# Key features times values: two heads a product, four chunks a burst, and the sums of keys made by transfers

## The chip, the cores and the metric

The kernel runs on one core of one Trainium2 chip. The metric is the device time of one execution in microseconds; the kernel before took 514.9 us, the median of three runs (514.82 to 515.21). The chip's engines run side by side, each through its own instructions in order: TensorE (PE) does matrix products, VectorE (DVE) and ScalarE (ACT) work element by element, GpSimd (POOL) does a little elementwise work and can issue transfers, and SyncE (SP) issues most of the transfers. SBUF is the on-chip memory with 128 partitions, PSUM the memory that TensorE writes into.

## The reference

Two branches share the input x (2048 rows of 512) and are mixed by a gate per row.

```python
pq, pk = per-head linear of q and k          # 32 heads of 16
phi_q = concat(softmax(pq), softmax(-pq))    # 32 features a head
phi_k = concat(softmax(pk), softmax(-pk))
kv  = einsum("bhsf,bhsd->bhfd", phi_k, v)    # a 32 x 16 matrix a head, summed over the 2048 rows
z   = einsum("bhsf->bhf", phi_k)             # the sum of the key features over the rows
num = einsum("bhqf,bhfd->bhqd", phi_q, kv)
den = einsum("bhqf,bhf->bhq", phi_q, z)[..., None] + 1e-6
a   = (num / den) @ wo
b   = relu(x @ w1 + b1) ** 2 @ w2 + b2       # 512 -> 1792 -> 512
out = g * a + (1 - g) * b,  g = sigmoid((x * gate_w).sum(-1))
```

The change is about `kv` and `z`, and about how the folded weights of the queries get back from a helper's layout.

## The kernel before

Rows come in 16 chunks of 128, four to a block, and the 1792 hidden units in 14 tiles. The program makes two sweeps over the four blocks, each with seven of the hidden tiles: 56 steps. A step is the up product of one hidden tile for 512 rows (`u`, 12 matmuls of 128x512), two steps ahead, and the down products of the present one (`d`, 12 matmuls). Every large product is three matmuls of split operands (high times high, high times low, low times high), all in one helper (lines 70 to 72).

The attention work is put between these steps by a table of slots (`at(slot, ...)`, two slots to a step); Tile's scheduler then orders each engine's instructions. In the first sweep each chunk has a projection `k` (with the key's per-head linear already folded into the weight), a softmax pair on DVE and ACT that leaves `phi` (128 rows x 1024 features) in a tile `e`, and a projection `v`, which ACT copies into `vext`: per head 16 values and a seventeenth column of ones. After every second chunk, `do_kv` runs a burst: per chunk and head one small matmul with 17 columns of `vext` as weights and 32 columns of `phi` streaming through, 32 of them a chunk, on the four 32-column strips of the PE array in turn. All chunks add into one PSUM bank `kvps`. The column of ones makes `z` in the same products: it is each head's seventeenth row.

After the last burst `kv_done` copies `kvps` out on DVE, sends the rows of `z` through DRAM so that they come back broadcast to all partitions (`zbc`, for the denominators on POOL in the second sweep), transposes the rest on PE (`kvt`) and writes it into `kvb`, the weights for the queries' numerators (`num`, line 400: 16 matmuls of 256 columns for each pair of chunks, on eight tiles of the array).

Besides, DVE folds the queries' per-head linear into their weight during the first sweep: 64 steps (`foldq_step`), each with a broadcast load `wqr` and a multiply-add into `row`; after every 16 steps DVE transposes the accumulated row (line 241) into a tile `wqt`, and at slot 46 four SP transfers with 512-byte pieces (line 245) write it into DRAM as `wqm`, from where four loads (line 249) bring the folded weights back. They are split into high and low parts (`wqh` on ACT, `wql` on DVE) for the first `q` projection right after the first sweep.

SP's transfers are issued in order: one that waits holds all behind it. So are the instructions of ACT and DVE.

Of the kernel before, what the change touches and what calls it, by code (L numbers as in the profile page):

```python
# [8 lines left out]
F32 = mybir.dt.float32  # L9
F32R = mybir.dt.float32r  # L10
AF = mybir.ActivationFunctionType
ALU = mybir.AluOpType
# [11 lines left out]
NFH = NF // 2  # L24
LAG = 2
NG = 8
VW = DH + 1
NV = 3
AHEAD = 150


# [1 line left out]
def tile_gated_mix(ctx: ExitStack, tc: tile.TileContext, xT, xn, wqT, wkT, wphi, wv, wo, w1, b1, w2, b2, gw, out):  # L33
# [110 lines left out]
    hold = pool("hold", NV)  # L144
# [15 lines left out]
    vext = [hold.tile([P, H * VW], F32, tag="vz", name=f"vext{i}") for i in range(NV)]  # L160
    heads = lambda v: v.rearrange("p (h v) -> p h v", v=VW)
    for v in vext:
        nc.gpsimd.memset(heads(v)[:, :, DH:VW], 1.0)
    zbc = []


# [59 lines left out]
    def foldq_step(i):  # L226
        g, e = divmod(i, DH)
        t = stage.tile([P, 512], F32, tag="in", name="wqr")
        nc.sync.dma_start(t, wqT.rearrange("(j e) g d -> g e j d", e=DH)[g, e].unsqueeze(1).to_broadcast([8, DH, D]))
        s = st["phc"][:, g, e:e + 1]  # L230
        with tc.issue_after(st["low"].ins):
            if e == 0:
                st["acc"] = row()
                nc.vector.tensor_scalar(st["acc"], t, s, None, ALU.mult)
            else:
                nc.vector.scalar_tensor_tensor(st["acc"], t, s, st["acc"], op0=ALU.mult, op1=ALU.add)  # L236
        if e == DH - 1:
            if g == 0:
                st["wqt"] = work.tile([P, 2, 4, NG, 32], F32, tag="phiT", name="wqt", bufs=1).rearrange(
                    "p u r g s -> p (u r g s)").rearrange("p (c g j) -> p c g j", c=4 * NK, g=NK)  # L240
            nc.vector.transpose(st["wqt"][:, :, g, :], st["acc"].rearrange("p (c j) -> p c j", c=4 * NK))

    def foldq_move():
        for r in range(4):
            nc.sync.dma_start(wqm.rearrange("c i (r n) -> r i c n", r=4)[r],
                              st["wqt"][32 * r:32 * r + 32].rearrange("p c g j -> p c (g j)"))
        st["wq"] = [row() for _ in range(NK)]
        for k in range(NK):
            nc.sync.dma_start(st["wq"][k], wqm[4 * k:4 * k + 4].rearrange("c i n -> (c i) n"))
# [43 lines left out]


    def gate_load(n):
        t = st["xn", n] = work.tile([P, D], F32, tag="ol" if n % 2 else "oh", name="xn", bufs=2)
        nc.sync.dma_start(t, xn[n])

    def gate_dot(n):
# [20 lines left out]
            mm3(ps, xs[k], ws[k], sc, ALL, k == 0, k == NK - 1)  # L320
        return ps

    def exps(ps, tag="e"):
# [4 lines left out]
        e = work.tile([P, H, 2, DH], F32, tag=tag, name="e", bufs=2 if tag == "e" else 1)  # L328
        bc = lambda t: t.unsqueeze(2).to_broadcast([P, H, DH])
        with tc.high_priority(offset=AHEAD):  # L330
            nc.vector.tensor_reduce(mx, pv, AX.X, ALU.max)
            nc.vector.tensor_reduce(mn, pv, AX.X, ALU.min)
            nc.vector.tensor_tensor(e[:, :, 0, :], pv, bc(mx), ALU.subtract)
            nc.vector.tensor_tensor(e[:, :, 1, :], bc(mn), pv, ALU.subtract)  # L334
# [13 lines left out]


    def kv_chunk(n, kvps, phi, v):  # L350
        for i in range(NG):
            for j in range(4):
                h = 8 * (i % 4) + 4 * (i // 4) + j
                nc.tensor.matmul(kvps[32 * j:32 * j + VW, 32 * i:32 * i + 32], v[:, h * VW:(h + 1) * VW],
                                 phi[:, 32 * h:32 * h + 32],
                                 start=(n == 0 and i == 0), stop=(n == NB * NC - 1),
                                 skip_group_check=True)

    def q_phi(n, e3, r):
        ez = work.tile([P, 2 * H, DH], F32, tag="ez", name="ez", bufs=1)  # L360
# [161 lines left out]
    def do_k(b, c):  # L522

        n = b * NC + c
        e3, r = exps(project(c, st["x", b], st["wa"], "k"), "ez" if n % NV == NV - 1 else "e")
        st["phi", n] = scaled(e3, r, nc.vector)

    def do_v(b, n, c):
        ps = project(c, st["x", b], st["wb"], "v")
        with tc.high_priority(offset=AHEAD):  # L530
            nc.scalar.activation(heads(vext[n % NV])[:, :, :DH], ps.rearrange("p (h f) -> p h f", f=DH), AF.Copy)

    def do_kv(n):
        if n == 0:
            st["kv"] = ps_b.tile([P, 2 * P], F32, tag="s", name="kvps")
        for m in (n, n + 1):
            kv_chunk(m, st["kv"], st["phi", m], vext[m % NV])

    def do_q(b, n, c):
        st["q", n] = exps(project(c, st["x", b], st["wa"], "q"))  # L540
# [8 lines left out]
        st["o", pair] = numer(st["pt", pair])  # L549

    def kv_done():
        kvps, kvs = st["kv"], row()[:, :2 * P]
        nc.gpsimd.memset(kvs, 0.0)
        for j in range(4):
            s = slice(32 * j, 32 * j + VW)
            with tc.high_priority(offset=AHEAD):
                nc.vector.tensor_copy(kvs[s, :], kvps[s, :])
        zr = zrow.rearrange("(i q j f) -> q j i f", i=4, q=2, f=32)
        for q in range(2):
            nc.sync.dma_start(zr[q], kvs[DH::32, q * P:(q + 1) * P].rearrange("p (i f) -> p i f", f=32))  # L560
        for half in range(2):
            z = hold.tile([P, H * VW], F32, tag="vz", name=f"z{half}")[:, :D]
# [7 lines left out]
        for j in range(4):  # L570
            s = slice(32 * j, 32 * j + 32)
            with tc.high_priority(offset=AHEAD):
                nc.vector.tensor_copy(kvb[s, :, DH * (j % 2):DH * (j % 2 + 1)], kt[s, :, :DH])

    def finish(n, c):
        ps = attended(st["o", n // 2], n % 2, st["wb"])
# [31 lines left out]
        at(5 + k // 2, v_ready, k)  # L608
    for b in range(NB):
        for c in range(NC):  # L610
            s = b * SL + 3 * c - 5 if b else 3
            at(s, gate_load, b * NC + c)
            at(s + 3 if b else 7 + c, gate_dot, b * NC + c)
            at(s + 5 if b else 9 + c, gate_chunk, b * NC + c)
        at(b * SL + 6, x_save, b)
        if b < NB - 1:
            at(b * SL + 4, x_fetch, b + 1)
# [2 lines left out]
        for c in range(NC):  # L620
# [13 lines left out]
    at(base + 11, do_w, wo, "o")  # L634
# [132 lines left out]
```

## Time and profile before

| What | Value |
|---|---|
| median of 3 runs | 514.9 us |
| the profiled execution's own time | 515.47 us |
| its span, first to last instruction | 513.7 us |
| PE busy | 509.4 us, 99% |
| DVE / ACT / POOL busy | 401.0 / 227.3 / 44.1 us |
| granted TensorE clock | 1.000 |
| moved by transfers | 75.35 MB, 147 GB/s |

The page shows one execution. A busy PE is not necessarily a PE at its peak, since the ends of its matmuls are modelled: what it really costs is read from the distances between starts. A row of the groups gives line, engine, operation, output and inputs, shapes and count, then the busy time and the mean length of one, then the idle time of the engine ahead of it and what ended that. A row of the timeline gives the start, the length and the count of instructions merged into it.

### The profile page before, as it was taken

The numbers are of one execution on the slowest core, as the hardware profiler recorded it, in microseconds if no ns is written. First come the engines' busy times: TensorE is split into PE (matmuls) and PEld (weight loads), VectorE is DVE, ScalarE is ACT, GpSimd is POOL, SyncE is SP. The second block draws the span as 40 slices with busy tenths as digits, with TensorE's granted clock in tenths as the row PEclk, the third lists the DMA queues.
The fourth block names the chain that finished last, engine by engine and source line by source line (L and its number), as shares of the span: only waits on it lengthen the run. The fifth ranks groups of instructions, "written<-read, shape, count | busy, mean of one in ns | idle before, by whom it ended". The sixth has DMA issues, their size and how long they took to land.

```text
span 513.7 us, 9257 instructions
## 1 busy us (share of the span) xinstructions
PE 509.4 (99%) x3536; PEld 411.3 (80%) x3536; DVE 401.0 (78%) x680; ACT 227.3 (44%) x390; POOL 44.1 (9%) x44
## 2 busy tenths in 40 slices
PE   9999999999999999999999999999999999999997
PEld 4888888888888888888888878788787878788876
DVE  3779769796998798787889787988779677797724
ACT  6676253254224344253854544242625353343530
POOL 1000000000000000000003040301111111201100
PEclk9999999999999999999999999999999999999999
DMA  8897535467554476548359152213153321032102
GB/s 300 290 329 236 160 119 161 142 210 245 201 157 147 156 255 223 189 139 225 107 167 342 40 163 77 92 42 103 35 167 106 85 77 48 3 101 82 41 24 82
DMA packets 48277, 75.35 MB, mean 147 GB/s; under 512 B 7016, under 2 KB 15464, under 8 KB 48232
## 3 DMA queue, kind: packets, MB, share of 16 engines
q1 hardware_dynamic: 47912, 74.35, 45.7%
q8 instruction: 28, 0.46, 0.4%
q10 hardware_dynamic: 288, 0.39, 0.2%
q14 instruction: 17, 0.14, 0.1%
q0 software_dynamic: 32, 0.01, 0.0%
HBM read 50.60 MB, written 17.83 MB: 133 GB/s over the span
## 4 chain that ended last, share of the span: by engine, by line
PE 98%; ACT 1%; DVE 0%; issue 0%
PE d L70 10%; PE u L70 10%; PE d L72 10%; PE d L71 10%; PE u L71 10%; PE u L72 10%; PE v L70 3%; PE k L70 3%; PE k L72 3%; PE q L70 3%; PE att L70 3%; PE q L71 3%; PE k L71 3%; PE att L72 3%; PE att L71 3%; PE q L72 3%
## 5 line engine op out<-in xcount | busy, mean ns | idle before, releaser
L435 ACT ACTIVATE r<-u,b1c 128x512 f32<-128x512 f32 x56 | 38.6, 689 | 163.0 <-PE u L72 162.6
L70 PE MATMUL d<-w2h,hh 128*128 128x512 f32 x222 | 86.7, 391 | 0.0
L72 PE MATMUL d<-w2h,hl 128*128 128x512 f32 x222 | 86.5, 389 | 0.0
L71 PE MATMUL d<-w2l,hh 128*128 128x512 f32 x222 | 86.4, 389 | 0.0
L70 PE MATMUL u<-xh,w1h 128*128 128x512 f32 x216 | 84.8, 393 | 0.0
L71 PE MATMUL u<-xl,w1h 128*128 128x512 f32 x216 | 84.1, 389 | 0.0
L72 PE MATMUL u<-xh,w1l 128*128 128x512 f32 x216 | 84.0, 389 | 0.0
L65 DVE TENSOR_TENSOR hl<-r,hh 128x512 fp32r<-128x512 f32 x56 | 37.8, 675 | 34.5 <-ACT hh L62 34.5
L339 DVE TENSOR_REDUCE sm<-e 128x64 f32<-128x1024 f32 x32 | 38.9, 1215 | 27.8 <-ACT e L336 27.8
L363 POOL TENSOR_TENSOR ez<-e,z 128x512 f32<-128x512 f32 x32 | 41.9, 1330 | 216.9 <-ACT e L336 210.8
L236 DVE SCALAR_TENSOR_TENSOR row<-wqr,phc,row 128x512 f32<-128x512 f32 x60 | 44.5, 742 | 6.6 <-DMA wqr<-in_wqT 6.2
L70 PEld LDWEIGHTS u<-xh,w1h 128*128 128x128 f32 x216 | 40.5, 188 | 11.1 <-issue 2.1
L70 PEld LDWEIGHTS d<-w2h,hh 128*128 128x128 f32 x222 | 41.7, 188 | 9.2 <-issue 0.6
L72 PEld LDWEIGHTS d<-w2h,hl 128*128 128x128 f32 x222 | 41.7, 188 | 8.7
L71 PEld LDWEIGHTS d<-w2l,hh 128*128 128x128 f32 x222 | 41.7, 188 | 8.6
L72 PEld LDWEIGHTS u<-xh,w1l 128*128 128x128 f32 x216 | 40.6, 188 | 8.5
L71 PEld LDWEIGHTS u<-xl,w1h 128*128 128x128 f32 x216 | 40.5, 188 | 8.2
L336 ACT ACTIVATE e<-e 128x1024 f32<-128x1024 f32 x32 | 33.8, 1057 | 24.0 <-DVE e L334 23.8
L387 ACT ACTIVATE phiT<-tb 32x256 f32<-32x256 f32 x64 | 26.5, 414 | 32.5 <-DVE tb L381 31.8
L62 ACT ACTIVATE hh<-r 128x512 fp32r<-128x512 f32 x56 | 35.3, 630 | 1.5
L436 ACT ACTIVATE r<-r 128x512 f32<-128x512 f32 x56 | 35.2, 628 | 1.1
L365 DVE TENSOR_REDUCE dz<-ez 128x64 f32<-128x1024 f32 x16 | 19.3, 1207 | 9.5 <-POOL ez L363 9.4
(116 smaller groups left out, 875.1 us busy)
## 6 DMA issues: line engine op xcount, KB each, us to landing
wqr<-in_wqT SPq DMA_DIRECT2D x64, 256.0 KB
in<-in_w SPq DMA_DIRECT2D x24, 256.0 KB
phiT<-tb SPq DMA_DIRECT2D x192, 32.0 KB
xin<-in_xT SPq DMA_DIRECT2D x16, 256.0 KB
xn<-in_xn SPq DMA_DIRECT2D x16, 256.0 KB
xkept<-xh SPq DMA_DIRECT2D x16, 256.0 KB
xkept<-xl SPq DMA_DIRECT2D x16, 256.0 KB
part<-row SPq DMA_DIRECT2D x16, 256.0 KB
```

The source lines that it names most:

```text
L62: i = nc.scalar.activation(hi, src, AF.Copy)
L65: st["low"] = elo.tensor_tensor(lo, src, hi.bitcast(F32), ALU.subtract)
L70: nc.tensor.matmul(o, ah[:, sa], bh[:, sb], start=first, stop=False)
L71: nc.tensor.matmul(o, ah[:, sa], bl[:, sb], start=False, stop=False)
L72: return nc.tensor.matmul(o, al[:, sa], bh[:, sb], start=False, stop=last)
L236: nc.vector.scalar_tensor_tensor(st["acc"], t, s, st["acc"], op0=ALU.mult, op1=ALU.add)
L336: nc.scalar.activation(ef, ef, AF.Exp)
L339: nc.vector.tensor_reduce(sm, e3, AX.X, ALU.add)
L363: nc.gpsimd.tensor_tensor(ez[:, hs, :], e3[:, hs, :], zbc[half], ALU.mult)
L387: nc.scalar.activation(dst, src, AF.Copy)
L435: nc.scalar.activation(r, ps, AF.Relu, bias=b1c[:, fc:fc + 1])
L436: nc.scalar.activation(r, r, AF.Square)
```

## The change

- **Products.** A small matmul now takes the values of two heads (32 columns, no column of ones) as weights and streams the features of the same two heads (64 columns in two pieces of 32). Half of the result, one head's values with the other head's features, is not used. A chunk has 16 of these instead of 32. `vext` becomes `val` (512 columns, with ACT's copy putting the head pairs side by side).
- **Bursts.** One burst after every fourth chunk instead of every second. For this five chunks' `phi` and `val` are kept instead of three: two more `e` tiles in the tile that the numerators use later (`ebig`), two more `val` tiles in the tag `ol`, which the gate's loads used (they now have two buffers instead of four, and other slots in the first block).
- **Sums of keys.** For chunks 0 to 14 a GpSimd transfer writes `phi` into the DRAM tile `zacc`, from chunk 1 on with an accumulating transfer (128 x 8 pieces of 512 bytes). At chunk 15 SP loads `zacc` into `zsum`, and behind the last burst `z_sum` multiplies `zsum` and the last `phi` by ones: eight matmuls with 256 columns into the other half of the PSUM bank.
- **Query fold.** Each quarter is transposed into a row of its own and stored right away by four GpSimd transfers with 128-byte pieces (16 in all). The four loads of `wqm` stay on SP.
- **After the bursts.** One DVE copy of the whole PSUM bank instead of four of 17 partitions, no `memset`, one transfer of `z` instead of two.

```diff
-VW = DH + 1
-NV = 3
+NV = 5
+    zacc = dram.tile([P, 2 * D], F32, name="zacc")
+    val = [hold.tile([P, D], F32, tag="vz", name=f"val{i}") for i in range(3)]
+    val += [work.tile([P, D], F32, tag="ol", name=f"val{i}", bufs=2) for i in range(3, NV)]
@@ foldq_step
-            nc.vector.transpose(st["wqt"][:, :, g, :], st["acc"].rearrange("p (c j) -> p c j", c=4 * NK))
-    def foldq_move():
-        for r in range(4):
-            nc.sync.dma_start(wqm.rearrange("c i (r n) -> r i c n", r=4)[r],
-                              st["wqt"][32 * r:32 * r + 32].rearrange("p c g j -> p c (g j)"))
+            t = row()
+            nc.vector.transpose(t, st["acc"])
+            for r in range(4):
+                nc.gpsimd.dma_start(wqm.rearrange("c i (r g j) -> r g i c j", r=4, g=NK)[r, g],
+                                  t[32 * r:32 * r + 32].rearrange("p (c j) -> p c j", j=32))
+    def foldq_load():
@@ kv_chunk
-        for i in range(NG):
+        ph = phi.rearrange("p (a g f) -> p a g f", a=4, f=2 * DH)
+        for i in range(4):
             for j in range(4):
-                h = 8 * (i % 4) + 4 * (i // 4) + j
-                nc.tensor.matmul(kvps[32 * j:32 * j + VW, 32 * i:32 * i + 32], v[:, h * VW:(h + 1) * VW],
-                                 phi[:, 32 * h:32 * h + 32],
+                m, g = i % 2, 4 * (i // 2) + j
+                nc.tensor.matmul(kvps[32 * j:32 * j + 32, 64 * i:64 * i + 64],
+                                 v[:, 64 * g + 32 * m:64 * g + 32 * m + 32], ph[:, 2 * m:2 * m + 2, g, :],
+    def z_keep(n):
+        nc.gpsimd.dma_start(zacc, st["phi", n], max_dma_last_dim=512, **({"accum_op": ALU.add} if n else {}))
+    def z_sum(kvps, parts):
+        one = nc.const_aps.tensor(1.0, (P, 32), F32)
+        for i, t in enumerate(parts):
+            for j in range(4):
+                nc.tensor.matmul(kvps[32 * j:32 * j + 32, 256:512], one, t[:, 256 * j:256 * j + 256],
+                                 start=i == 0, stop=i == len(parts) - 1, skip_group_check=True)
@@ do_k
+        if n < NB * NC - 1:
+            z_keep(n)
+        else:
+            st["z"] = work.tile([P, 2 * D], F32, tag="tb", name="zsum", bufs=2)
+            nc.sync.dma_start(st["z"], zacc)
@@ do_kv
-        for m in (n, n + 1):
-            kv_chunk(m, st["kv"], st["phi", m], vext[m % NV])
+        for m in range(n, n + 4):
+            kv_chunk(m, st["kv"], st["phi", m], val[m % NV])
+        if n == NB * NC - 4:
+            z_sum(st["kv"], (st["z"], st["phi", n + 3]))
@@ the table of slots
-            if c % 2:
-                at(s + 5, do_kv, n - 1)
+            if c == NC - 1:
+                at(s + 4.5, do_kv, n - 3)
-    at(46, foldq_move)
+    at(46, foldq_load)
```

**The last burst, on PE.** `kvps` is the PSUM bank of the small products, `u` and `d` the up and down products, `kvt` the transposes of `kv_done`. Before:

```order
L72 MATMUL u<-xh_3_2649,w1l_2532 128x512
L354 MATMUL kvps<-e,vext_113 17x32 x32
L354 MATMUL kvps<-e,vext_111 17x32 x32
L70 MATMUL d_2493<-w2h_645,hh 128x512
L71 MATMUL d_2493<-w2l_646,hh 128x512
```

and now, at the same place:

```order
L71 MATMUL u<-xh_3_2482,w1l_2364 128x512
L355 MATMUL kvps<-e,val_114 32x64 x16
L355 MATMUL kvps<-ebig,val_115 32x64 x16
L355 MATMUL kvps<-ebig,val_116 32x64 x16
L355 MATMUL kvps<-e,val_112 32x64 x16
L370 MATMUL kvps<-zsum,const-float32-1.0 32x256 x4
L370 MATMUL kvps<-e,const-float32-1.0 32x256 x4
L69 MATMUL d_2325<-w2h_645,hh 128x512
L70 MATMUL d_2325<-w2l_646,hh 128x512
L71 MATMUL d_2325<-w2h_645,hl 128x512
L69 MATMUL d_2326<-w2h_645,hh 128x512
L595 MATMUL kvt<-ident,row 128x128 x2
```

A burst has 64 small matmuls as before, now for four chunks, and the last one has eight of 256 columns behind it; `kvt` stands four matmuls behind the burst, where eight stood before.

**The end of the first sweep, on DVE.** `sm` and the scaled `e` belong to the last chunk's `phi`, `wql` is the split of the folded query weights, `wol` that of the output weights, `hl` the hidden units' low part. Before:

```order
L339 TENSOR_REDUCE sm<-e 128x64
L65 TENSOR_TENSOR hl<-r,hh 128x512
L341 RECIPROCAL r<-sm 128x64
L303 SCALAR_TENSOR_TENSOR xn,lg<-xn,gwb 128x512
L345 TENSOR_TENSOR e<-e,r 128x1024
L65 TENSOR_TENSOR w1l_2870<-in,w1h_2869 128x512
L65 TENSOR_TENSOR w2l_2876<-in,w2h_2875 128x512
L65 TENSOR_TENSOR wql_2864<-row,wqh_2863 128x512
```

and now:

```order
L339 TENSOR_REDUCE sm<-e 128x64
L64 TENSOR_TENSOR hl<-r,hh 128x512
L64 TENSOR_TENSOR wql_2635<-row,wqh_2634 128x512
L64 TENSOR_TENSOR wql_2677<-row,wqh_2676 128x512
L341 RECIPROCAL r<-sm 128x64
L64 TENSOR_TENSOR wql_2693<-row,wqh_2692 128x512
L345 TENSOR_TENSOR e<-e,r 128x1024
L299 SCALAR_TENSOR_TENSOR xn,lg<-xn,gwb 128x512
L64 TENSOR_TENSOR wql_2801<-row,wqh_2800 128x512
```

Three of the four splits of the query weights now stand ahead of the last `phi`, not behind it.

**The end of GpSimd's transfers and SP's issue behind them, in the changed kernel** (POOL; before, it had no transfer here):

```order
L364 DMA zacc<-e 128x8x128
L364 DMA zacc<-ebig 128x8x128
L239 DMA wqm<-row 32x16x32 x2
L364 DMA zacc<-ebig 128x8x128
L239 DMA wqm<-row 32x16x32 x2
```

The last transfer of `phi` (chunk 14) stands between the halves of the fold's last quarter. On SP the load of `zsum`, two loads of `wo` and then the four loads of `wqm` stand behind it, and then the other loads of `wo`. DVE's copy of `kv_done` stands behind the split of the third tile of `wo`.

More of the change, by code (lines that the diff above doesn't have):

```diff
@@ L295, in gate_load @@
     def gate_load(n):
-        t = st["xn", n] = work.tile([P, D], F32, tag="ol" if n % 2 else "oh", name="xn", bufs=2)
+        t = st["xn", n] = work.tile([P, D], F32, tag="oh", name="xn", bufs=2)
         nc.sync.dma_start(t, xn[n])
@@ L321, in project, with e_tile, exps @@
         return ps
-    def exps(ps, tag="e"):
+    def e_tile(tag, bufs):
+        return work.tile([P, H, 2, DH], F32, tag=tag, name="e", bufs=bufs)
+    def exps(ps, e=None):
         pv = ps.rearrange("p (h f) -> p h f", f=DH)
@@ L327, in exps @@
         mn = small.tile([P, H], F32, tag="mn", name="mn")
-        e = work.tile([P, H, 2, DH], F32, tag=tag, name="e", bufs=2 if tag == "e" else 1)
+        if e is None:
+            e = e_tile("e", 2)
         bc = lambda t: t.unsqueeze(2).to_broadcast([P, H, DH])
@@ L524, in do_k @@
         n = b * NC + c
-        e3, r = exps(project(c, st["x", b], st["wa"], "k"), "ez" if n % NV == NV - 1 else "e")
-        st["phi", n] = scaled(e3, r, nc.vector)
+        i = n % NV
+        if n == 3:
+            big = work.tile([P, 2, 4, NG, 32], F32, tag="phiT", name="ebig", bufs=1)
+            st["ebig"] = big.rearrange("p u r g s -> p (u r g s)")
+        if i < 2:
+            e = e_tile("e", 2)
+        elif i == 2:
+            e = e_tile("ez", 1)
+        else:
+            e = st["ebig"][:, (i - 3) * 2 * D:(i - 2) * 2 * D].rearrange("p (h t f) -> p h t f", t=2, f=DH)
+        e3, r = exps(project(c, st["x", b], st["wa"], "k"), e)
+        st["phi", n] = scaled(e3, r, nc.vector)
+        if n < NB * NC - 1:
+            z_keep(n)
+        else:
+            st["z"] = work.tile([P, 2 * D], F32, tag="tb", name="zsum", bufs=2)
+            nc.sync.dma_start(st["z"], zacc)
     def do_v(b, n, c):
@@ L551, in kv_done @@
     def kv_done():
[L552 to L560, printed above, removed]
+        kvs = row()
+        with tc.high_priority(offset=AHEAD):
+            nc.vector.tensor_copy(kvs, st["kv"])
+        nc.sync.dma_start(zrow.rearrange("(j f) -> j f", j=4), kvs[::32, 256:512])
         for half in range(2):
-            z = hold.tile([P, H * VW], F32, tag="vz", name=f"z{half}")[:, :D]
+            z = hold.tile([P, D], F32, tag="vz", name=f"z{half}")
             nc.sync.dma_start(z, zrow[half * D:(half + 1) * D].partition_broadcast(P))
```

23 lines of the change are left out of this document (9 added, 14 removed).

## The prediction

> **What bounds the kernel now.** I read the page first: busy shares, slices and the chain.
>
> ```profile
> span 513.7 us, 9257 instructions
> PE 509.4 (99%) x3536; PEld 411.3 (80%) x3536; DVE 401.0 (78%) x680; ACT 227.3 (44%) x390; POOL 44.1 (9%) x44
> POOL 1000000000000000000003040301111111201100
> DMA  8897535467554476548359152213153321032102
> PE 98%; ACT 1%; DVE 0%; issue 0%
> ```
>
> PE is busy 99% of the span and is 98% of the chain that ended last; it waits for nobody for long. So work taken off PE shortens the time one for one, and a change on another engine costs only if PE then waits. POOL does nothing in the first sweep (slices 2 to 21), and the transfer engines are nowhere full after the start.
>
> Since busy PE is not PE at its peak, I price PE's work by distances between starts, from timelines of PE around three bursts (columns: start, length, engine, line). The first burst of the key features with the values:
>
> ```profile
> 59.62 0.39 PE L70 MATMUL d<-w2h,hh 128*128 128x512 f32 x1
> ...
> 60.75 0.39 PE L72 MATMUL d<-w2h,hl 128*128 128x512 f32 x1
> 61.07 1.27 PE L354 MATMUL kvps<-e,vext 128*17 128x32 f32 x128
> 62.31 0.47 PE L70 MATMUL v<-wvh,xh 128*128 128x512 f32 x1
> 62.62 0.39 PE L71 MATMUL v<-wvl,xh 128*128 128x512 f32 x1
> ```
>
> From 59.62 to 60.75 are five ordinary steps: 0.2267 us each (the rows round it). From 60.75 to 62.62 are 1.87, less two ordinary steps of 0.453: **the burst costs 1.42 us**. The last one:
>
> ```profile
> 255.81 0.39 PE L72 MATMUL u<-xh,w1l 128*128 128x512 f32 x1
> 256.12 1.32 PE L354 MATMUL kvps<-e,vext 128*17 128x32 f32 x128
> 257.37 0.50 PE L70 MATMUL d<-w2h,hh 128*128 128x512 f32 x1
> 257.71 0.39 PE L71 MATMUL d<-w2l,hh 128*128 128x512 f32 x1
> ```
>
> 1.90 - 0.453 = 1.45. Seven bursts of 1.42 and this one make **11.4 us**.
>
> **The change on PE.** The groups of the small products (busy, mean of one):
>
> ```profile
> L354 PE MATMUL kvps<-e,vext 128*17 128x32 f32 x1024 | 10.2, 196 | 0.0
> L354 PEld LDWEIGHTS kvps<-e,vext 128*17 128x17 f32 x1024 | 9.2, 96 | 2.8 <-issue 2.8
> ```
>
> A burst's 64 products are 128 records, two for each. In the first burst the last record of some 0.19 us ends the 1.27, so 128 records start within 1.08 us: 8.5 ns from one to the next, and on each of the four strips of the array a record every 34 ns. What remains, 1.42 - 1.09 = 0.33, is the price of going into a burst and out of it. Four bursts instead of eight save four such prices, 1.3 us, whatever the records do.
>
> A new record streams 64 columns instead of 32. The trace has no such record, so I bound it. A wide burst is that of the numerators, 32 records of 256 columns on eight tiles, four after each other on a tile:
>
> ```profile
> 303.92 0.39 PE L72 MATMUL d<-w2h,hl 128*128 128x512 f32 x1
> 304.24 1.09 PE L400 MATMUL num<-phiT,kvb 64*32 64x256 f32 x32
> 305.26 0.50 PE L70 MATMUL u<-xh,w1h 128*128 128x512 f32 x1
> 305.60 0.40 PE L71 MATMUL u<-xl,w1h 128*128 128x512 f32 x1
> ```
>
> 1.68 - 0.453 = 1.23; less 0.33, and over four, that is 0.224 us for 256 columns on one tile. With 34 ns for 32 columns this gives 0.85 ns a column and 7 ns a record, so 61 ns for 64 columns. Lower bound: columns alone, a quarter of 0.224 = 56 ns. Upper bound: two old records, 68 ns. A strip has 32 records a burst, so a burst costs 0.33 + 32 x 0.061 = **2.28** (2.12 to 2.51), four bursts 9.1 (8.5 to 10.0).
>
> Added: `z_sum`, eight products of 256 columns = 16 records, four after each other on each strip, inside the last burst, so without a new price of entry: 4 x 0.224 = **0.9**. They have 128 rows and not 64; four strips of 128 rows run beside each other in L354 already.
>
> Sum: 9.1 + 0.9 - 11.4 = **-1.4 us** (-2.0 to -0.5). The profiled execution took 515.47 with its span of 513.7, so its span would be about 512.3 and its own time 514.1; the median of the runs lies 0.6 lower, and 514.9 - 1.4 = **513.5 us**.
>
> `kvt` now stands four steps (0.9 us) behind the burst. DVE's copy of 512 columns ahead of it is like the passes over 512 columns out of PSUM below, 0.68. It fits into the 0.9 within about 0.2 us, and I leave that in the range.
>
> **The change off PE.** DVE loses four copies and gains one; ACT's copy of `v` has the same 512 columns; SP loses transfers. All of it lies beside PE. Fifteen transfers of 512 KB add 7.9 MB to 75 MB, at times when the transfer slices read 4 to 7 of 10. What matters is the end of the first sweep, where PE waits for what GpSimd's transfers deliver. The trace has one of them:
>
> ```profile
> L148 POOL DMA_DIRECT2D b1c<-in_b x1 | 0.7, 699 | 0.3 <-issue 0.3
> b1c<-in_b POOLq DMA_DIRECT2D x1, 7.0 KB, 4.8
> ```
>
> It issues for 0.70 us and lands 4.8 after its start, 4.1 after its issue ended. It has 128 pieces, one a partition; `phi`'s transfer has 1024, one of the fold 512. Lower bound: 0.70 each, whatever the count. Upper bound: in proportion, 5.6 and 2.8. The timelines of the end of the sweep (DVE, SP, ACT):
>
> ```profile
> 231.78 0.70 DVE L241 STREAM_TRANSPOSE wqt<-row 128x512 f32<-128x512 f32 x1
> 233.40 1.22 DVE L345 TENSOR_TENSOR e<-e,r 128x1024 f32<-128x1024 f32 x1
> 241.72 0.68 DVE L334 TENSOR_TENSOR e<-mn,k 128x512 f32<-128x512 f32 x1
> 247.11 1.22 DVE L345 TENSOR_TENSOR e<-e,r 128x1024 f32<-128x1024 f32 x1
> ...
> 221.24 1.12 SPq L80 DMA_DIRECT2D in<-in_w  x2
> ...
> 232.51 3.14 SPq L245 DMA_DIRECT2D wqm<-wqt  x4
> ...
> 239.66 1.75 SPq L249 DMA_DIRECT2D row<-wqm  x4
> ...
> 248.96 8.36 SPq L286 DMA_DIRECT2D in<-in_wo  x16
> ...
> 223.99 0.63 ACT L62 ACTIVATE w1h<-in 128x512 fp32r<-128x512 f32 x1 [0.47 <-DMA in<-in_w]
> ```
>
> Chunk 14's `phi` is ready at 234.6, the fold's last quarter at 232.5; GpSimd then issues two stores of the fold, `phi`, and two stores, in this order. SP used to get its four `wqm` loads off at 239.66.
>
> By the lower bound the last store is issued at 234.6 + 3 x 0.7 = 236.7 and lands at 240.8, about when the loads went off before: nothing is late. By the upper bound: two stores from 232.5 to 238.1, `phi` to 243.7, two stores to 249.3, landed at 253.4. When is it late? SP then needs 1.75 for the four loads and, at 8.36 / 16 = 0.52 each, about 6 for ten pieces of `wo` and two of x; a load lands 2.75 after its issue (221.24 to 223.99); `woh`, `wol` and `hl` are some 2 us more, and then DVE can copy the sums. The old burst starts at 256.12; the new one comes 1.4 sooner against chunk 14, since three bursts (6.8 us) stand before it instead of seven (9.9), and three instead of six (8.5) before chunk 14. Its end, 254.7 + 2.28 + 0.9 = 257.9, less the 12.5 us above, gives **245.4 as the latest landing without a wait**, 10.8 us after `phi`. The lower bound is 4.6 sooner, the upper 8.0 later. I take no wait: the point midway, 247.1, is late by under 2 us, and the old kernel's stores were through in 7 us (232.51 to 239.66).
>
> **The rivals.**
>
> *GpSimd's transfers are late at the sweep's end.* A mechanism that ends on the other side: `wqm` lands after 245.4, SP holds `wo` behind it, ACT and DVE hold `woh`, `wql`, the last `phi`, and PE waits ahead of the last burst or of `kvt`. Price: each microsecond past 245.4, up to 8.0; with 3 as its likeliest, 516.5 us. From 1.4 us on it eats the gain. For it: in proportion is the natural reading of an engine that writes pieces one by one, and the queue behind is long. Against it: the 0.7 us may be mostly fixed, and the up products, whose `hl` DVE would hold back, run two steps ahead of the down products that need it.
>
> ```profile
> L234 DVE TENSOR_SCALAR row<-wqr,phc 128x512 f32<-128x512 f32 x4 | 1.9, 479 | 0.0
> L236 DVE SCALAR_TENSOR_TENSOR row<-wqr,phc,row 128x512 f32<-128x512 f32 x60 | 44.5, 742 | 6.6 <-DMA wqr<-in_wqT 6.2
> ```
>
> The Trainium skill (SBUF — State Buffer, in "SBUF: two separate sides") adds that such a transfer's list cannot be written while DVE runs one of its fast two-port copies. Of the fold's passes only the four of L234 are that quick for 512 columns (479 ns beside 742), so by that rule they would add under 2 us in all; no run here shows it.
>
> *The accumulating transfers are slower than the chunks come.* Then they pile up and `zsum` comes late by all the sum.
>
> ```profile
> 61.14 1.20 PE kvps L354 x82
> 89.75 1.20 PE kvps L354 x82
> ```
>
> In the chain of waits two chunks take 28.6 us, one 14.3. If a transfer, with its wait for the one before, took 18, fifteen would be 55 us over, less the 20 from chunk 14's `phi` (234.6) to the last burst (254.7): about 548 us with the gain. Against it: the four stores of the fold, 1 MB in pieces of 512 bytes, went from 232.51 to 239.66 at most, 3.6 us for 512 KB; reading the sum as well would make that 7.
>
> *The products are paced by their weights.* The weights have 32 columns instead of 17; if 8.5 ns a record is the load of 17 columns, 32 take 16: 128 x 0.016 + 0.33 = 2.38 a burst, -1.0 in all, 513.9; with 17 ns (twice the old) 2.51 and -0.5, 514.4.
>
> For this rival speaks a rule of the Trainium skill (TensorE: Matmul & The Clock Gate, Part 3 on packing small matmuls), that a weight load overlaps running products only on another row group, which the four strips here are not. This trace disagrees at 17 columns: 128 loads of 96 ns each (the second row of the groups above) lie within 1.27 us.
>
> **How the numbers follow.** This kernel tells 0.2% (1.0 us) from no change. No wait, -1.4 us: chance 0.48, of it faster 0.40, same 0.08 (the sum's upper end). GpSimd late: 0.36, of it faster 0.02, same 0.12, slower 0.22. Weights: 0.10, of it faster 0.03, same 0.07. Transfers pile up: 0.06, slower. Faster 0.45, same 0.27, slower 0.28. The likeliest has its own range of 512.9 to 514.4. The range is 512.9 to 518.5: below, the sum's lower end; above, GpSimd late by 5 us; outside stay the pile-up and the worst of the lateness.
>
> **What would show it.** In the changed profile: the four bursts cost 2.1 to 2.5 each and the last 0.9 more; the chain stays at 98% PE; POOL's transfers show issue times that say which bound holds; the loads of `wqm` on SP go off before 245. Wrong if PE has a gap ahead of the last burst, of `kvt` or of the first `q`, or if a record of 64 columns starts later than 17 ns after the one before.

## The result, and the profile after

The changed kernel takes **539.0 us** (median of four runs, 537.5 to 539.8) beside 514.9 before: a ratio of 1.046, interval 1.044 to 1.049. The forecast was 513.5, with a range up to 518.5.

The page of the changed kernel: span, busy shares, the chain by engine, the fold's pass (L236 is now L234) and a new group of DMA issues (last number: us to landing).

```profile
span 535.7 us, 8357 instructions
...
PE 514.6 (96%) x3040; PEld 414.3 (77%) x3040; DVE 401.2 (75%) x677; ACT 227.1 (42%) x390; POOL 76.8 (14%) x71
...
PE 68%; DMA 16%; DVE 10%; issue 2%; ACT 2%; SPq 0%; DVEq 0%; ACTq 0%
...
L234 DVE SCALAR_TENSOR_TENSOR row<-wqr,phc,row 128x512 f32<-128x512 f32 x60 | 44.7, 745 | 30.4 <-DMA wqr<-in_wqT 30.0
...
zacc<-e POOLq DMA_DIRECT2D x9, 512.0 KB, 11.5
```

PE is down from 98% of the chain to 68%; transfers and DVE have 26%. DVE's work is what it was (401 us), but its wait for `wqr`, the broadcast weight rows that the fold multiplies, went from 6.2 us to 30.0. PE waits four times for over 2 us, and never did before (waits by engine: who, for what, us in total, times, longest):

```profile
PE v L69 <- DVE e L334: 6.8, 1, 6.8
PE kvt L595 <- DVE row L586: 4.6, 1, 4.6
PE d L69 <- DVE row L742: 2.6, 1, 2.6
PE v L69 <- DVE ebig L334: 2.1, 1, 2.1
```

**How a late `wqr` stops PE.** The largest of them, from the timelines of DVE and PE:

```profile
127.90 0.75 DVE L234 SCALAR_TENSOR_TENSOR row<-wqr,phc,row 128x512 f32<-128x512 f32 x1 [2.39 <-DMA wqr<-in_wqT]
128.57 0.69 DVE L64 TENSOR_TENSOR hl<-r,hh 128x512 fp32r<-128x512 f32 x1
134.24 0.75 DVE L234 SCALAR_TENSOR_TENSOR row<-wqr,phc,row 128x512 f32<-128x512 f32 x1 [4.99 <-DMA wqr<-in_wqT]
134.91 0.68 DVE L331 TENSOR_REDUCE mx<-k 128x32 f32<-128x512 f32 x1
...
136.71 0.68 DVE L334 TENSOR_TENSOR e<-mn,k 128x512 f32<-128x512 f32 x1
...
130.37 0.39 PE L71 MATMUL u<-xh,w1l 128*128 128x512 f32 x1
137.53 0.76 PE L69 MATMUL v<-wvh,xh 128*128 128x512 f32 x1 [6.77 <-DVE e L334]
138.09 0.63 PE L70 MATMUL v<-wvl,xh 128*128 128x512 f32 x1
138.52 0.63 PE L71 MATMUL v<-wvh,xl 128*128 128x512 f32 x1
```

DVE works in order. It stands 5 us at a fold step whose `wqr` has not landed. Behind that step are the four passes that read `k` out of PSUM. In the first sweep `project` has a single bank, since the other holds the burst sums, so `v` cannot start until L334 has read `k`. The fold is work beside PE in time, but stands ahead of PE's next input in DVE's queue. The gaps ahead of `d` and `v` at 223.9 and 229.0 come about in the same way: DVE waits for `wqr` three times from 216.5 to 222.4 (2.0, 1.4 and 0.8 us), and the passes that free the banks for `d` (L742) and `v` (L334) stand behind.

**What the transfers looked like there.** Windows of 5 us: the next to last number is the busy share of 16 transfer engines (packets overlap, so it can pass 1), the third from last the clock granted to PE. First the kernel before:

```profile
110.00:115.00 5.00, 5.00 (x24) 4.14 (x23) 5.00 (x9) 1.28 (x3) 0.00 (x0) 1.00 0.86 278
125.00:130.00 5.00, 5.00 (x24) 4.14 (x23) 2.54 (x5) 1.96 (x3) 0.00 (x0) 1.00 0.52 197
```

The changed kernel:

```profile
110.00:115.00 5.00, 5.00 (x24) 4.14 (x23) 5.00 (x10) 0.55 (x2) 2.68 (x4) 1.00 1.14 248
125.00:130.00 5.00, 5.00 (x24) 4.14 (x23) 1.87 (x3) 1.47 (x3) 0.00 (x0) 1.00 1.18 254
135.00:140.00 5.00, 2.47 (x6) 2.02 (x7) 5.00 (x9) 2.52 (x4) 0.00 (x0) 0.50 0.53 177
140.00:145.00 5.00, 5.00 (x16) 3.90 (x15) 4.10 (x7) 1.07 (x3) 1.59 (x1) 0.63 0.59 183
```

In the window of before at 125, SP issues nothing but `wqr` loads, six back to back (SP's timeline of before):

```profile
121.95 11.17 SPq L229 DMA_DIRECT2D wqr<-in_wqT  x6
```

The share is 0.52. **That is not half idle, it is this load's full speed.** Counted from the trace's packet records, it moves some 98 pieces of 2048 bytes a microsecond there, at 84 ns each: eight engines' worth. The Trainium skill states the reason (DMA: Bandwidth & Descriptors, "Rules for kernel authors"): the size of the outermost dimension caps the number of engines, and `wqr`'s is 8. The trace agrees: 98 times 84 ns a microsecond is 8.2 engines.

Beside a sum's transfer the load falls to 55 to 60 pieces a microsecond, as from 130 to 136 in the changed kernel. There the sum's own pieces of 512 bytes come at some 60 a microsecond, 64 ns each; with `wqr`'s, now 98 ns each, that is some nine engines' worth of recorded time, so how the one slows the other is not shown.

The last two windows show a second price. Behind the 6.8 us gap the granted clock reads 0.50 and 0.63, and thirteen products start 0.427 us apart instead of 0.227, 3.0 us more in all with their neighbours. Over the whole run, PE's waits come to 17.9 us where the undisturbed no_sums_few_wqr below has 1.6, and PE is busy for 514.6 us instead of 506.9. The Trainium skill (TensorE: Matmul & The Clock Gate, Part 1) says that half clock follows an idle window of about 3.4 us. The trace agrees for the gaps of 6.8 and 4.6 us, but not for a third stretch of half clock, 3.4 us from 229.0 on: the gap ahead of it is 2.1 us, with one of 2.6 us 3 us before that. In no_sums below, gaps of 2.0 and 2.1 us without such a neighbour leave the clock at 1.00.

**The products did better than forecast.** The second and the last of the four bursts on PE:

```profile
151.21 0.39 PE L71 MATMUL u<-xh,w1l 128*128 128x512 f32 x1
151.53 0.65 PE L355 MATMUL kvps<-ebig,val 128*32 128x64 f32 x32
152.00 1.52 PE L355 MATMUL kvps<-e,val 128*32 128x64 f32 x96
153.45 0.50 PE L69 MATMUL d<-w2h,hh 128*128 128x512 f32 x1
153.79 0.40 PE L70 MATMUL d<-w2l,hh 128*128 128x512 f32 x1
...
269.43 0.39 PE L71 MATMUL u<-xh,w1l 128*128 128x512 f32 x1
...
272.54 0.50 PE L69 MATMUL d<-w2h,hh 128*128 128x512 f32 x1
272.88 0.40 PE L70 MATMUL d<-w2l,hh 128*128 128x512 f32 x1
```

By the prediction's measure a burst costs 153.79 - 151.21 - 0.453 = 2.13 us (the first three alike), and the last, with the sums, 3.00. Three of 2.13 and one of 3.00 are 9.4 instead of 11.3: **1.9 us less on PE**, where 1.4 was forecast.

**The end of the sweep.** GpSimd, SP, ACT, DVE and PE from the last sum on:

```profile
251.38 1.59 POOL L364 DMA_DIRECT2D zacc<-ebig  x1 [1.01 <-ACT w2h L61]
252.30 1.99 POOL L239 DMA_DIRECT2D wqm<-row  x2
...
259.83 0.33 SPq L555 DMA_DIRECT2D zsum<-zacc  x1
260.25 0.85 SPq L282 DMA_DIRECT2D in<-in_wo  x2
261.32 1.78 SPq L245 DMA_DIRECT2D row<-wqm  x4
...
270.35 0.69 DVE L64 TENSOR_TENSOR wql<-row,wqh 128x512 fp32r<-128x512 f32 x1
270.96 0.68 DVE L64 TENSOR_TENSOR w2l<-in,w2h 128x512 fp32r<-128x512 f32 x1
...
271.71 4.40 SPq L282 DMA_DIRECT2D in<-in_wo  x8
...
275.65 0.63 ACT L61 ACTIVATE woh<-in 128x512 fp32r<-128x512 f32 x1 [1.31 <-DMA in<-in_wo]
...
276.31 0.69 DVE L64 TENSOR_TENSOR wol<-in,woh 128x512 fp32r<-128x512 f32 x1 [2.01 <-ACT woh L61]
...
277.52 0.68 DVE L586 COPY row<-kvps 128x512 f32<-128x512 f32 x1
...
278.35 0.66 PE L595 MATMUL kvt<-ident,row 128*128 128x128 f32 x2 [4.60 <-DVE row L586]
```

This is the chain of the first rival: `wqm`, then SP's queue with `wo`, then ACT and DVE, then `kvt`. It goes through DVE twice: the last eight pieces of `wo` go off at 271.71 because SP waits 2.9 us for the split `w2l`, which stands in DVE's queue behind the splits `wql` of the late `wqm`. The gap ahead of `kvt` took 4.6 us of the 24.

### The profile page after: what moved, and what is told of

Same layout as the page of the kernel before. It is cut to its first block, busy times and chain, and to the rows that moved or that the text cites. A ratio compares the mean times of both kernels' runs of the same rounds, so it can differ in the third digit from the quotient of the medians.

```text
span 535.7 us, 8357 instructions
## 1 busy us (share of the span) xinstructions
PE 514.6 (96%) x3040; PEld 414.3 (77%) x3040; DVE 401.2 (75%) x677; ACT 227.1 (42%) x390; POOL 76.8 (14%) x71
## 3 DMA queue, kind: packets, MB, share of 16 engines
q0 software_dynamic: 15248, 8.92, 13.4%
## 4 chain that ended last, share of the span: by engine, by line
PE 68%; DMA 16%; DVE 10%; issue 2%; ACT 2%; SPq 0%; DVEq 0%; ACTq 0%
DMA wqr<-in_wqT 12%; PE d L69 7%; PE d L70 7%; PE d L71 7%; PE u L69 7%; PE u L70 7%; PE u L71 7%; PE q L69 3%; PE q L71 3%; PE q L70 3%; PE att L70 3%; PE att L69 3%; PE att L71 3%; DMA in<-in_w 3%; DVE row L234 2%
## 5 line engine op out<-in xcount | busy, mean ns | idle before, releaser
L70 PE MATMUL d<-w2l,hh 128*128 128x512 f32 x222 | 87.6, 394 | 0.0
L234 DVE SCALAR_TENSOR_TENSOR row<-wqr,phc,row 128x512 f32<-128x512 f32 x60 | 44.7, 745 | 30.4 <-DMA wqr<-in_wqT 30.0
L339 DVE TENSOR_REDUCE sm<-e 128x64 f32<-128x1024 f32 x26 | 31.6, 1217 | 22.3 <-ACT e L336 22.2
L336 ACT ACTIVATE e<-e 128x1024 f32<-128x1024 f32 x26 | 27.5, 1056 | 25.0 <-DVE e L334 24.7
L69 PE MATMUL v<-wvh,xh 128*128 128x512 f32 x64 | 27.1, 423 | 8.9 <-DVE e L334 6.8
## 6 DMA issues: line engine op xcount, KB each, us to landing
zacc<-e POOLq DMA_DIRECT2D x9, 512.0 KB, 11.5
```

Source lines behind the costliest of these rows:

```text
L69: nc.tensor.matmul(o, ah[:, sa], bh[:, sb], start=first, stop=False)
L70: nc.tensor.matmul(o, ah[:, sa], bl[:, sb], start=False, stop=False)
```

## The experiments

Theory A says that the sums' transfers take engines from `wqr`, DVE stands at the fold, and PE stands behind DVE. B blames the fold's stores on GpSimd, in pieces of 128 bytes. C says that the loss comes from the end of the sweep alone.

### Leaving the sums out: no_sums

```diff
-        nc.gpsimd.dma_start(zacc, st["phi", n], max_dma_last_dim=512, **({"accum_op": ALU.add} if n else {}))
+        if n == 0:
+            nc.gpsimd.dma_start(zacc, st["phi", n], max_dma_last_dim=512)
```

> The changed kernel with the fourteen accumulating transfers left out (zacc keeps chunk 0 alone, so the denominators are wrong; all else stays, the fold's stores on GpSimd too). Theory A, that the accumulating transfers take the transfer engines from the fold's loads wqr, which hold DVE and through it PE: no PE gap in the first sweep, wqr waits back under 10 us (from 30.0), granted clock 1.000, 513.5 to 515 us. Theory B, that the fold's stores in pieces of 128 bytes do it: 535 us or more. Theory C, that it is the chain of waits at the sweep's end alone (GpSimd's stores, wqm, wo): the gap of 4.8 us ahead of kvt stays, about 519.

520.1 us, ratio 1.010 (1.007 to 1.013): the fourteen transfers account for 18.9 us of the 24. B is left with 5 us at most, since the fold's stores are all there. The time is nearer to C's than to A's, but C's sign is missing: the gap ahead of `kvt` is 0.9 us. And 520 is not 513: DVE still waits 15.3 us for `wqr`, and PE still has gaps ahead of `v` from 131.2 and 217.6 on, of 2.0 and 2.1 us.

### Sums that don't add: plain_sums

```diff
-        nc.gpsimd.dma_start(zacc, st["phi", n], max_dma_last_dim=512, **({"accum_op": ALU.add} if n else {}))
+        nc.gpsimd.dma_start(zacc, st["phi", n], max_dma_last_dim=512)
```

> The changed kernel with each of phi's transfers a plain write of the same pieces to the same place instead of an accumulating one (the sums of keys are those of chunk 14 and 15 only, so the denominators are wrong). Pieces and bytes written are the same, the reading of the old sum is gone. If the adding is what is dear (65 ns a piece of 512 bytes against 36 ns for such pieces of the old fold's store): a piece takes about 36 ns, and the time falls by about half of the loss, 524 to 530. If the traffic or the packets' number is what counts: within 3 us of the changed kernel.

529.9 us, ratio 1.029 (1.022 to 1.035). The mere traffic costs 10, the adding 9, both give or take 3, since the two runs lie at 527.0 and 532.8. One thing changed besides: the trace shows the plain transfers' 512-byte pieces joined into 4096-byte packets.

### The size of the pieces: big_pieces

```diff
-        nc.gpsimd.dma_start(zacc, st["phi", n], max_dma_last_dim=512, **({"accum_op": ALU.add} if n else {}))
+        nc.gpsimd.dma_start(zacc, st["phi", n], **({"accum_op": ALU.add} if n else {}))
```

> The changed kernel, its accumulating transfers in pieces of the default size (up to 4096 bytes) instead of 512. Theory A1 (an accumulating transfer costs by its pieces: 65 ns for each of 64 pieces on an engine, 4.2 us): with an eighth of the pieces an engine is taken for under 2 us, and the time falls to the plain transfers' 527 to 531 us or below. Theory A2 (it costs by its bytes, since each byte is read, added and written back): 536 to 541 us, no change.

538.7 us, ratio 1.045 (1.044 to 1.047), the time of 512-byte pieces; against plain_sums, whose packets have the same size, the adding costs 9 us by itself (6 to 12 by plain_sums' two runs). The queue line of the page (share of 16 engines' span; 13.4% in the changed kernel, 5.4% in plain_sums):

```profile
q0 software_dynamic: 2704, 8.92, 9.3%
```

The big pieces hold the engines for less time and land sooner (7.9 us instead of 11.5), yet `wqr` waits no less (34.3 us). Recorded engine time is therefore not the price; why not, these runs don't tell.

### The fold's stores back on SP: fold_sp

```diff
-                nc.gpsimd.dma_start(wqm.rearrange("c i (r g j) -> r g i c j", r=4, g=NK)[r, g],
+                nc.sync.dma_start(wqm.rearrange("c i (r g j) -> r g i c j", r=4, g=NK)[r, g],
```

> The changed kernel with the fold's sixteen stores issued by SP instead of GpSimd, the same pieces of 128 bytes. Theory A: the loss stays, 535 to 541 us, or grows by the time that SP's queue stands behind these stores. Theory B or C with GpSimd's issue as the cause: 514 to 525.

537.3 us, ratio 1.043 (1.041 to 1.045). B falls: which queue issues the fold's stores is worth some 2 us (537.3 beside 539.0), and no_sums_few_wqr below has all these stores on GpSimd and takes 513.2.

### All sixteen engines for wqr: wqr_copies_first

The factors meet other rows, so the query weights come out wrong; bytes and passes are the same.

```diff
-        nc.sync.dma_start(t, wqT.rearrange("(j e) g d -> g e j d", e=DH)[g, e].unsqueeze(1).to_broadcast([8, DH, D]))
+        nc.sync.dma_start(t, wqT.rearrange("(j e) g d -> g e j d", e=DH)[g, e].unsqueeze(0).to_broadcast([DH, 8, D]))
```

> The changed kernel with the fold's broadcast loads written as 16 copies of 8 rows instead of 8 rows of 16 copies each: the same bytes with the same sizes, but the outermost count is 16 instead of 8 (the rows then meet the wrong factors, so the folded query weights are wrong). In the trace a wqr load alone moves 98 packets of 84 ns in a microsecond, as much as 8 of 16 engines can. Theory A in the form that those 8 engines are overfull (per chunk of 14.3 us: 8.2 for wqr, some 3.4 for other loads, 4.2 for the sums): twice the rate for wqr, its waits under 10 us, 513.5 to 518. If instead the accumulating pieces hold up every engine: 530 or more.

529.2 us, ratio 1.029 (1.026 to 1.031), with nothing about the sums changed. DVE's wait for `wqr` falls from 30.0 to 18.4 us, not under 10 as A expected. Speeding up the load that the sums disturb takes back 10 us, and not all.

### The sums on the kernel before: before_with_sums

```diff
         st["phi", n] = scaled(e3, r, nc.vector)
+        if n < NB * NC - 1:
+            nc.gpsimd.dma_start(zacc, st["phi", n], max_dma_last_dim=512, **({"accum_op": ALU.add} if n else {}))
```

> The kernel before, with nothing changed but fifteen added transfers of the finished key features into DRAM, issued by GpSimd as in the changed kernel (512-byte pieces, fourteen of them accumulating); nobody reads what they add up to. Theory A (these transfers take the transfer engines from the loads of the fold's weight rows, wqr; DVE stands at L236-like steps, and the next projection waits for DVE): the same loss without any change of the products, by the difference of 19 us between the changed kernel and the one without its sums: 528 to 536 us, with gaps of PE ahead of a v near 130 and 220. Rival D (the loss needs the new schedule of the products, four chunks a burst, which brings PE earlier to the chunks between bursts): 515 to 518 us, PE still at 99%.

526.5 us, ratio 1.022 (1.020 to 1.024), between the two expectations and near A's. The fold's pass in its page:

```profile
L237 DVE SCALAR_TENSOR_TENSOR row<-wqr,phc,row 128x512 f32<-128x512 f32 x60 | 44.8, 747 | 21.6 <-DMA wqr<-in_wqT 21.2
```

The sums cost 11.3 us with the old products and 18.9 with the new. So the mechanism does not need the new products, but it is dearer with them. One reason shows in the starts of `v`. That of chunk 7 stands at 133.28 in the kernel before and at 130.80 in no_sums_few_wqr below, where nothing is late: with fewer bursts behind it PE comes sooner. In no_sums, with all `wqr` loads, it stands at 133.27, and the lead is lost. This is not the whole reason: `v` of chunk 13 starts at 219.72 in no_sums and at 216.53 before, so there `wqr` is later than it was. SP issues the last six loads ahead of it from 203.97 on, where the kernel before issues seven from 197.11 on; what holds SP back, the gate's new slots or the order of its queue, no run here separates.

### wqr sixteen engines wide, without sums: no_sums_wqr16

The right factors come as a small input in the matching order; columns are put in order when the weights are split.

```diff
-        nc.sync.dma_start(t, ...[g, e].unsqueeze(1).to_broadcast([8, DH, D]))
+        nc.sync.dma_start(t, ...[g, e].unsqueeze(0).to_broadcast([DH, 8, D]))
...
-            nc.vector.transpose(t, wph)
-            nc.vector.tensor_reduce(st["phc"], t.rearrange("p (g j e) -> p g e j", g=NK, e=DH), AX.X, ALU.add)
+        nc.sync.dma_start(st["phc"], wphq)
```

> The changed kernel without its fourteen accumulating transfers (the sums of chunks 1 to 14 are left out, so denominators are wrong), and with wqr loaded in an order that puts it on all 16 transfer engines instead of 8 (copies outermost; its factors come from a 32 KB input in the matching order, and the fold's columns are put right when the weights are split). Theory A: what no_sums still loses against the sum of the products (520.1 against 514.9 - 1.9 = 513.0) is also wqr coming late, since four bursts take 1.9 us less and PE arrives earlier at chunks whose loads are paced by 8 engines. Then the gaps of PE at 130, 213 and 216 close: 512.6 to 514.5 us, DVE's wait for wqr under 7 us. Rival D (what is left comes from the new slots of the gate's loads, the two buffers of xn, or the order of the queues): 517.5 to 520.5 us, the gaps stay.

516.5 us (514.4 to 521.7 in twelve runs), ratio 1.004 (1.001 to 1.006), between the theories. The wait for `wqr` falls from 15.3 to 9.1 us and two of the twelve runs reach A's range, but most don't. Even in the profile, of one of these two, the load moves some 195 pieces a microsecond only for three microseconds from 122 on, and from 126 to 131 51 to 104. There a piece takes 120 to 300 ns on average instead of 84, since some take several hundred, with nothing else of size in the trace. What slows them is open.

### A quarter of the loads: few_wqr and no_sums_few_wqr

DVE runs the same passes, but four in a row use one tile, so three quarters of the fold's weight rows are left out.

```diff
-        t = stage.tile([P, 512], F32, tag="in", name="wqr")
-        nc.sync.dma_start(t, wqT...)
+        if i % 4 == 0:
+            st["wqr"] = stage.tile([P, 512], F32, tag="in", name="wqr")
+            nc.sync.dma_start(st["wqr"], wqT...)
+        t = st["wqr"]
```

> The changed kernel with all its sums, but only every fourth of the 64 loads of wqr: four steps of the fold take the same tile, so three quarters of the fold's weight rows are left out and the query weights are wrong. DVE runs the same passes. Theory A (the sums' transfers cost time through wqr alone): the gaps ahead of v close and what is left is the gap ahead of kvt, 4 to 5 us: 516.5 to 519 us. Rival F (the sums' transfers also hold up the loads of x, of the weights or of the gate by themselves): 524 us or more.

> The same with the fourteen accumulating transfers left out as well. Theory A: nothing is late, and the sum on PE is all that is left of the change: 514.9 - 1.9 = 513.0 us, 512.6 to 513.6, in all its runs, with PE's gaps under 1 us in all. Rival D (part of no_sums' 520 us comes from the gate's slots and buffers or from the queues' order): 515 us or more.

Without sums: **513.21 us** (513.01 to 513.44 in five runs), ratio 0.9964 (0.9951 to 0.9977). The page:

```profile
span 511.7 us, 8207 instructions
...
PE 506.9 (99%) x3040; PEld 409.5 (80%) x3040; DVE 400.6 (78%) x677; ACT 227.0 (44%) x390; POOL 54.4 (11%) x57
```

This is PE's part of the change alone, with its 1.9 us less and a gap of 0.6 ahead of `kvt`; the time is 0.4 us less than these two make it, and why isn't shown. Rival D falls as a cost of its own: with `wqr` on time, the new gate slots and buffers cost nothing.

With all sums: 520.3 us, ratio 1.0095 (1.0078 to 1.0112), 1.3 us above A's range. (The loads left out are 12.6 MB of traffic as well. I put the relief down to `wqr`, since the three gaps of the changed kernel ahead of `v` and `d` led to it.) No gap ahead of `v` is over 0.4 us; what stays is the end of the sweep. Its rows (ACT, DVE, and PE's wait; lines stand two or three lower than in the changed kernel):

```profile
245.58 0.63 ACT L61 ACTIVATE wqh<-row 128x512 fp32r<-128x512 f32 x1 [4.03 <-DMA row<-wqm]
...
246.24 0.69 DVE L64 TENSOR_TENSOR wql<-row,wqh 128x512 fp32r<-128x512 f32 x1 [3.44 <-ACT wqh L61]
...
PE kvt L597 <- DVE row L588: 5.0, 1, 5.0
```

ACT's wait of 4.0 us for `wqm` says little by itself, since no_sums_few_wqr has one of 4.1 there and no such gap. The difference is when SP gets the four loads of `wqm` off: 10.7 us ahead of the last burst here (241.95 and 252.67), 17.0 there (235.23 and 252.23).

The rest of the 7 us over 513.2 is mostly the slower clock behind that gap: PE is busy 509.4 us instead of 506.9.

### The load that reads the sums: zsum_gpsimd and few_wqr_zsum_gpsimd

SP stood 5.3 us at the load of `zsum`, with `wo` and `wqm` behind it.

```diff
-            nc.sync.dma_start(st["z"], zacc)
+            nc.gpsimd.dma_start(st["z"], zacc)
```

> The changed kernel, with the one load that reads the sums back (zsum) issued by GpSimd instead of SP. Theory Z (the gap of 4.8 us ahead of kvt: SP stands 5.3 us at that load, which waits for the last accumulating transfer, and the loads of wo and of the folded weights queue behind it on SP): the gap falls under 2 us and the time to 534 to 536.5 us. Rival B2 (the folded weights are late by themselves, since their stores lie beside the last sums): SP then stands at the loads of wqm instead, the gap stays, 537.5 to 540 us.

> Both edits: a quarter of the wqr loads, and zsum loaded by GpSimd; all sums are made. Theories A and Z together: both ways in which the sums cost time are gone, 512.8 to 514.5 us. If one of them falls it shows here too: 516 to 519 us if the gap ahead of kvt stays.

541.8 us (537.4 to 543.6), ratio 1.051 (1.046 to 1.056), and 520.1 us (518.7 to 522.3), ratio 1.010 (1.007 to 1.014). The gap ahead of `kvt` stays at 4.4 and 5.2 us. Theory Z falls. SP now stands at the next load in its queue (waits and timeline of zsum_gpsimd):

```profile
SPq L245 <- DMA wqm<-row: 2.9, 1, 2.9
...
262.38 1.77 SPq L245 DMA_DIRECT2D row<-wqm  x4
```

The stores of `wqm` that lie beside the last sum are late by themselves: the last of them lands at 262.29, 8.0 us after its start, where the two ahead of the sum take 2.2.

### Sums by GpSimd: group_sums_wqr16

A complete kernel: `wqr` as in no_sums_wqr16, and GpSimd adds four chunks up in place behind their burst, so that only two sums go to DRAM.

```diff
+    def z_group(n):
+        t = st["phi", n + 3]
+        for m in range(n, n + 3):
+            nc.gpsimd.tensor_tensor(t, t, st["phi", m], ALU.add)
+        if n < 8:
+            nc.gpsimd.dma_start(zacc, t, max_dma_last_dim=512, **({"accum_op": ALU.add} if n else {}))
```

> A version that computes everything: GpSimd adds up the key features of four chunks in place behind their burst (three adds of 128x1024 a group), two partial sums go to DRAM (one plain, one accumulating transfer) and come back in the last block, and wqr comes on 16 engines. Theory A: no transfers beside wqr but two, so PE's gaps close and the products' saving is left: 512.8 to 514.5 us. Rival E (GpSimd's adds slow DVE, which shares its side of the SBUF by the Trainium skill, SBUF - State Buffer; here 13 adds of about 2.6 us by the 1.31 us of a 128x512 one): DVE's passes beside an add take visibly longer than 1.22 us and PE waits again: 515 to 519 us.

537.8 us, ratio 1.043 (1.040 to 1.047): one bound is given up for another. GpSimd's adds and DVE's passes beside them:

```profile
90.07 8.99 POOL L365 TENSOR_TENSOR ebig<-ebig,e 128x1024 f32<-128x1024 f32 x3 [87.35 <-DVE row L229]
...
91.24 2.76 DVE L229 SCALAR_TENSOR_TENSOR row<-wqr,phc,row 128x512 f32<-128x512 f32 x1
...
93.99 2.82 DVE L294 SCALAR_TENSOR_TENSOR xn<-xn,gwb 128x512 f32<-128x512 f32 x1
...
100.92 0.74 DVE L229 SCALAR_TENSOR_TENSOR row<-wqr,phc,row 128x512 f32<-128x512 f32 x1
```

A pass that takes 0.74 us alone takes 2.8 beside an add; DVE is busy 425.5 us instead of the 400.7 of no_sums_wqr16, and PE waits for it 10.2 us ahead of `v`. Rival E's mechanism holds; its price, 515 to 519, was far too low. No complete version that we ran beats the kernel before.

## Why the prediction was wrong

**The PE sum was right.** Without the sums' transfers and with a quarter of the `wqr` loads, the changed kernel takes 513.2 us, inside the likeliest case's own range of 512.9 to 514.4. The terms: a burst measured 2.13 (forecast 2.28, bounds 2.12 and 2.51). Its 128 records run from 151.53 to 153.52; less the last one's 0.22, they start 14 ns apart, 56 on a strip, the lower bound "columns alone", so the 7 ns a record that I added were not there. `z_sum` measured 3.00 - 2.13 = 0.87 (forecast 0.9). `kvt` was held 0.6 us even there, where I left 0.2. That the cheaper bursts (0.5 us in all) and this gap (0.4) cancel is luck.

**The step that failed** is "All of it lies beside PE" for the fifteen transfers, at "times when the transfer slices read 4 to 7 of 10". I put their price for PE at nothing. The kernel before's slices there read 3 to 8, and one behind them 9; but the reading failed for another reason: I took a mean over sixteen engines for room. For a load confined to eight, 0.5 is full, and the sums take some 40% of its speed away (98 pieces a microsecond fall to 55 to 60; by what mechanism is open). The second half of the error is that I had quoted the fold's row with 6.2 us of waits for `wqr`, and read it only for the length of DVE's passes. It said that this load was already just in time. I never asked what stands behind the fold step in DVE's queue: L331 to L334, and behind them, by the single bank, PE.

What it cost, from four runs that differ in sums and loads:

| | all `wqr` loads | a quarter of them |
|---|---|---|
| without sums | 520.1 | 513.2 |
| with sums | 539.0 | 520.3 |

Against 513.2, late `wqr` costs 6.9 us with no sums at all, in part by PE's new pace; the sums cost 7.1 with hardly any `wqr`, at the sweep's end; both together cost 25.8, 11.8 more than the two added.

**Rival 1** (GpSimd late at the sweep's end) happened by its mechanism, and its price, up to 8.0 us, holds the 4.6 of the gap; but it was not GpSimd's issue that made it. GpSimd issues a sum in 1.5 to 1.6 us and the fold's stores in 1.1 on average, much nearer the flat bound than the proportional one. What is late is the landing: 8.4 us for the last sum (11.5 at the median), 7.8 and 7.5 for the stores behind it, where the two ahead of it took 2.2. My latest landing was too generous as well: the last store lands 9.7 us and `wqm`'s loads go off 10.5 us behind chunk 14's `phi` (ready at 250.8), within the 10.8 that I allowed, and `kvt` still waits, because the last eight pieces of `wo` go off only at 271.71, behind `w2l`, and not right behind the first at half a microsecond each. It cost 4.6 us of gap, to which the slower clock adds; few_wqr shows 7.1 for this end of the sweep in all. That alone would have put the time near 520, above the range.

**Rival 2** (the sums pile up) did not happen: a sum lands in 11.5 us at the median, within the 14.3 of a chunk, and the three slowest, 14.6 to 14.9 us, were through before the next was issued. The price in engine time that I argued against it, 3.6 or 7 us for 512 KB, was never the question. I checked the sums against themselves and not against their neighbours.

**Rival 3** (products paced by their weights) is out: 14 ns a record, below the 16 or 17 that it needed.

## What to carry to other kernels

Before adding traffic beside a bound engine, look for the load that is already awaited, however briefly, and follow the queue of the engine that waits: a wait of 6 us that costs nothing is a line with no slack left. Read a transfer share against the engines that the load in question can use, not against all of them. And work taken off the bound engine brings it sooner to everything that was just on time.

## What the hardware showed that was not expected

- An accumulating 512 KB transfer costs its neighbours more than its recorded engine time tells: 13.4% and 9.3% of the engines' span for small and large pieces end in the same 539 us, and plain writes at 5.4% in 530. Why is open.
- A gap of PE costs more than itself: 3.0 us of half clock behind one of 6.8.
- DVE's scalar_tensor_tensor on 128x512 takes 2.8 us instead of 0.74 beside a GpSimd add of SBUF operands. The Trainium skill (SBUF — State Buffer, "SBUF: two separate sides") calls the shared ports an exclusive lock for passes with two SBUF inputs against such an add, and the run agrees.
- With its copies outermost, the same load runs at some 195 pieces a microsecond instead of 98, but only for stretches; in others a piece takes 120 to 300 ns on average instead of 84, with no other traffic of size in the trace.
